# State reads in 128×32 tiles and a turn per half, batch 1 by seven half products, the scale vector loaded as rows, and the whole instruction order written anew

## The chip, the cores and the metric

One core of a Trainium2 chip. The metric is the device time in microseconds of one execution. Five engines work side by side, each through its own instructions in order: TensorE (PE, with its weight loads listed as PEld), VectorE (DVE), ScalarE (ACT), GpSimd (POOL) and SyncE (SP, which here only issues DMAs).

## The reference, cut to what matters

```python
def _attn_ref(x, state):                     # x: (8, 8, 512, 64), state: (8, 8, 32, 64)
    scores = scale * np.matmul(x, state.transpose(0, 1, 3, 2))
    a = softmax(scores)                      # over the 32 states of a head
    xread = np.matmul(a, state)
    scores2 = scale * np.matmul(state, x.transpose(0, 1, 3, 2))
    a2 = softmax(scores2)                    # over the 512 tokens
    sread = np.matmul(a2, x)
    return np.concatenate([xread, sread], axis=2)

def _moe_ref(x, w_in, w_out, alpha):         # x: 8*544 rows of 512
    h = x @ w_in                             # to 2048
    g = np.maximum(h, 0.0) + alpha * np.minimum(h, 0.0)
    return g @ w_out                         # back to 512
```

Inputs and output are float32. The output has 4352 rows of 512: for each of 8 batches 512 token rows and then 32 state rows.

## The kernel before, in words

The kernel is a list of steps in a fixed order. `ORDER` is a string of tokens such as `F.3.12.0`; the loop at the end splits each at its dots and calls the step of that name. An engine runs its instructions in the order in which the tokens issue them, so the string is a schedule of all engines at once. Nothing is planned at run time. The tokens end in an engine letter (`a` ACT, `v` DVE, `p` POOL) where a step can run on several, and in PSUM bank numbers where a step opens a bank.

**Attention.** Per batch `b`, x is loaded in f16 (`lx`, line 157, on POOL's DMA queue; batch 0 in float32 on SP's queue and cast, `cx`), transposed (`xd` by DMA, or `xt` on PE and `xo` out of PSUM), and the scores of all 8 heads are made in 64×32 tiles of the PE (`sc`, line 303). The softmax over the states is `sb`, `smax`, `ssh`, `sexp`, `ssum`, `snorm`, `wb`; for batch 0 it goes by halves, with `tsc`, `at` and `ao` around it. The softmax over the tokens is `tm`, `nb`, `te`, `tsum`, `tn`, then a DMA transpose `tt`. The state rows are loaded and transposed by `lst`, `stc`, `stt`, `sto`, `sbd`, `str`, `sro`. `rd` (line 467) then makes the state reads of a batch: 32 matmuls with x as the stationary operand (128 rows, 64 columns) and 32 columns of weights moving, two column halves of the PE in turn; `rdo` copies them into `XS`, the moving operand of the state rows' first product.

**MLP.** The first product is folded with the attention: `m` (line 494) makes state times w_in per batch and quarter of d_ff, and `F` (line 543; `f` line 565 for half batches) multiplies it by the attention weights, giving 128 rows of h for 512 tokens. "Batch 8" stands for the 256 state rows of all batches; its `F.8` (line 552) takes `XS`. `N` (lines 596 and 580, ACT) and `G` (lines 599 and 584, DVE) are the activation: ACT makes relu(-h), DVE adds (1 - alpha) times it to h. `oma` makes 1 - alpha.

**The second product** is done in two ways. Batches 0 and 1 go straight: `S` (line 613) is two matmuls of 512 columns, 32 such steps per batch, and `O` copies a finished 128×512 block out. Batches 2 to 7 and 8 go by seven half products instead of eight: `W` (line 656, POOL) makes four differences of w_out's quarters once, `U` (line 680, POOL) makes four sums of g's halves per batch in two pieces each, `P` (line 701) is four matmuls of 256 columns, 28 such steps per batch, `K` keeps a partial result out of PSUM, and `Q` (lines 732 and 734) adds or copies a quarter of the output and sends it off.

`Z` (line 223) is `fill`: matmuls on a constant pattern whose result is not used. `x_out`, `states_out`, `tokens_out` and the other copies take their engine from the token.

Of the kernel before, what the change touches and what calls it, by code (L numbers as in the profile page):

```python
# [8 lines left out]
F32 = mybir.dt.float32  # L9
F16 = mybir.dt.float16  # L10
# [11 lines left out]
xt.1.1.1.0 xt.1.0.0.3 wo.3 te.0.1 tsum.0 xo.1.0.0.v oma mo.0.0.a.0 m.1.0 f.0.1.0.4 sexp.0.1 ssum.0.1 xo.1.1.1.v  # L22
mo.1.0.a n.0.1.0 xt.1.0.1.1 xo.1.0.1.v f.0.0.0.2 n.0.0.0 xt.1.1.0.5 xo.1.1.0.v g.0.1.0.1 g.0.1.0.0 m.2.0.3.0 m.1.1
mo.1.1.a snorm.p.0.1 at.1.1 mo.2.0.a.0 ao.1.v g.0.0.0.1 m.0.1.5.4 mo.0.1.a.0 sc.1 tm.1 f.0.1.1.1 f.0.0.1.3 mo.0.1.a.1
F.0.4.5 F.0.5.4 mo.2.0.a.1 n.0.0.1 nb.1.a n.0.1.1 sb.1 te.1.0 g.0.0.0.0 g.0.1.1.0 te.1.1 S.0.2.1.0 g.0.1.1.1 F.0.6.2
N.0.6 g.0.0.1.1 g.0.0.1.0 tsum.1 G.0.6 N.0.5 G.0.5 S.0.2.0 S.0.1.1.1 m.0.2 mo.0.2.a F.0.7.3 N.0.7 smax.1 S.0.1.0 N.0.4
G.0.4 F.0.10.2 N.0.10 m.0.3 G.0.7 mo.0.3.a F.0.11.4 G.0.10 N.0.11 G.0.11 F.0.9.5 m.1.3 N.0.9 G.0.9 F.0.13.3 N.0.13
tn.0.1.p F.0.8.2 S.0.1.5 F.0.12.4 S.0.3.1.5 S.0.2.5 N.0.8 G.0.13 N.0.12 ssh.p.1 wo.1 sexp.1 F.0.15.3 S.0.3.5 G.0.8
S.0.2.4 mo.1.3.a G.0.12 ssum.1.2 F.0.14.4 S.0.2.6 S.0.1.6 m.1.2 S.0.3.6 S.0.3.4 snorm.v.1 lx.2 xd.2 wb.1 tn.1.1.a
S.0.1.4 W.1.1.p S.0.2.2 S.0.1.3 F.1.3.2 tn.0.0.a tt.0 mo.1.2.a N.0.14 S.0.2.3 G.0.14 N.0.15 G.0.15 F.1.10.4 F.1.2.3  # L30
tn.1.0.p N.1.3 G.1.3 N.1.2 G.1.2 S.0.2.7 O.0.2.a tt.1 S.0.3.0 N.1.10 F.1.4.2 N.1.4 G.1.10 G.1.4 S.0.1.7 F.1.9.0
F.1.11.3 N.1.9 G.1.9 F.1.1.4 N.1.1 G.1.1 S.0.1.2 N.1.11 W.3.0.p G.1.11 S.0.3.2 F.1.6.2 N.1.6 S.0.3.7 O.0.1.a sc.2 tm.2
m.2.2.0.4 rd.0.3 mo.2.2.a.1 sb.2 mo.2.2.a.0 rdo.0.a F.1.15.1 N.1.15 W.1.0.p G.1.15 nb.2.a S.0.0.5.4 F.1.8.0 N.1.8
G.1.8 G.1.6 te.2.0 S.0.0.2 S.0.0.1 te.2.1 S.0.0.4 W.2.0.p lx.3 F.1.7.3 smax.2 ssh.p.2 F.1.14.1 F.1.5.0 S.0.0.7 F.1.0.2
W.4.0.p N.1.14 G.1.14 N.1.7 N.1.5 S.0.3.3 G.1.7 N.1.0 G.1.0 m.3.2 F.1.13.1 mo.3.2.a S.0.0.0 F.1.12.3 S.0.0.3 G.1.5
xd.3 S.0.0.6 S.1.1.2.2 S.1.0.2.0 N.1.13 G.1.13 N.1.12 tsum.2 sexp.2 O.0.0.a G.1.12 S.1.0.4 S.1.0.0 ssum.2.1 snorm.v.2
wb.2 O.0.3.a m.2.3.3.4 mo.2.3.a.1 m.2.1 mo.2.1.a S.1.0.3 S.1.1.4 mo.2.3.a.0 tn.2.0.p S.1.1.5 W.2.1.p m.3.3.5.4
# [62 lines left out]
def kernel(  # L100
# [47 lines left out]
    def engine(e):  # L148
        return nc.gpsimd if e == "p" else nc.vector

    live = {}
    xgs = {}
    x0s = []

    def load_x(b):
        xg = xgs[b] = att.tile([128, H, 2, 2, D], F16, name=f"xg_{b}", tag="xg", bufs=3)
        nc.gpsimd.dma_start(
            xg.rearrange("p k j r d -> p k j (r d)"),
            x[b].rearrange("k (j p r) d -> p k j (r d)", j=2, r=2),
        )  # L160
# [625 lines left out]
```

## Time and profile before

| what | value |
|---|---|
| device time, median of 3 | 214.17 us (214.09 to 214.41) |
| span of the profiled execution, first to last instruction | 212.2 us |
| PE busy | 203.6 us, 1974 matmuls |
| DVE busy | 174.8 us, 260 instructions |
| ACT busy | 150.3 us, 292 instructions |
| POOL busy | 165.0 us, 106 instructions |

The page gives one span, 212.2 us; the profiled execution's own device time is not listed beside it, so the 1.9 us between the span and the median stand here for what lies around a span. "Busy" is the time in which an engine has at least one instruction running. Matmuls overlap in the array, so the busy time of PE can be full while it waits; the chain view, which gives the time from one piece to the next, tells more.

### The profile page before, as it was taken

What the parts mean: (1) busy time and instruction counts of PE and PEld (TensorE: products, weight loads), DVE (VectorE), ACT (ScalarE), POOL (GpSimd) and SP (SyncE); (2) the same over time, 40 slices, a digit from 0 to 9 for tenths busy, and PEclk for the clock granted to TensorE, in tenths of its full rate; (3) what the DMA queues carried; (4) which work ended last, traced back from release to release, by engine and by line L of the source; (5) the groups of instructions that cost most, each with busy time, mean ns of one, the idle gap of its engine ahead of it and who ended that gap; (6) DMA issues with size and microseconds to landing.
All of it is one profiled execution on the core that took longest, in us unless ns stands there. A gap on an engine that the chain in (4) does not pass through costs nothing.

```text
span 212.2 us, 4985 instructions
## 1 busy us (share of the span) xinstructions
PE 203.6 (96%) x1974; PEld 132.5 (62%) x1974; DVE 174.8 (82%) x260; ACT 150.3 (71%) x292; POOL 165.0 (78%) x106
## 2 busy tenths in 40 slices
PE   7989899989999999999999999999999999999993
PEld 5655234444444545766668776767777678888882
DVE  0789999889999999999999999899997997423221
ACT  2489998789999869987998578878773866312110
POOL 8343074946749898969989999799979995999960
PEclk9999999999999999999999999999999999999999
DMA  6999979879599299634115581141305200121142
GB/s 172 208 183 205 207 114 163 127 186 114 172 111 258 29 150 149 151 78 123 53 49 57 95 249 48 21 131 21 82 8 145 102 0 0 53 99 49 43 158 99
DMA packets 52438, 23.68 MB, mean 112 GB/s; under 512 B 38464, under 2 KB 51392, under 8 KB 52416
## 3 DMA queue, kind: packets, MB, share of 16 engines
q0 software_dynamic: 18816, 8.09, 30.2%
q1 hardware_dynamic: 33328, 15.22, 28.5%
q8 instruction: 15, 0.25, 0.4%
q10 hardware_dynamic: 272, 0.07, 0.1%
q14 instruction: 7, 0.06, 0.1%
HBM read 17.31 MB, written 8.91 MB: 124 GB/s over the span
## 4 chain that ended last, share of the span: by engine, by line
PE 86%; DVE 6%; ACT 4%; DMA 2%; issue 1%; POOL 0%; POOLq 0%; ACTq 0%; DVEq 0%; SPq 0%
PE h L543 23%; PE px L701 21%; PE o L613 11%; PE pv L701 10%; PE py L701 5%; PE m_ps L494 4%; PE fill L223 4%; PE h L552 3%; PE sr_ps L467 2%; DMA e2T<-e 2%; DVE mx L368 1%; DVE g L599 1%; ACT m L520 1%; PE sc L303 1%; PE xT_ps L288 1%; ACT neg L596 1%
## 5 line engine op out<-in xcount | busy, mean ns | idle before, releaser
L599 DVE SCALAR_TENSOR_TENSOR g<-neg,oma_sb,h 128x512 f16<-128x512 f32 (+1 forms) x140 | 92.5, 710 | 9.5 <-ACT neg L596 8.3
L596 ACT ACTIVATE neg<-h 128x512 f32<-128x512 f32 (+1 forms) x140 | 75.3, 583 | 22.3 <-PE h L543 13.3
L543 PE MATMUL h<-aT,m 128*128 128x512 f16 x248 | 67.7, 379 | 1.3 <-DVE g L599 0.6
L701 PEld LDWEIGHTS <-gsum 128*128 128x128 f16 x416 | 40.3, 98 | 11.5 <-issue 1.3
L543 PEld LDWEIGHTS <-m 128*128 128x128 f16 x248 | 23.4, 98 | 20.1 <-issue 3.3
L701 PEld LDWEIGHTS <-g 128*128 128x128 f16 x312 | 30.3, 98 | 8.7 <-issue 0.8
L680 POOL TENSOR_TENSOR gsum<-g,g 128x1024 f16<-128x1024 f16 (+1 forms) x14 | 27.8, 1986 | 7.1 <-DVE g L599 4.8
L613 PE MATMUL o<-w_out_sb,g 128*128 128x512 f16 x128 | 33.1, 379 | 0.0
L680 POOL TENSOR_TENSOR gsum<-g,gsum 128x1024 f16<-128x1024 f16 (+1 forms) x14 | 27.8, 1991 | 1.9 <-PE px L701 1.6
L680 POOL TENSOR_TENSOR gsum<-g 128x1024 f16<-128x1024 f16 (+1 forms) x14 | 27.7, 1993 | 1.9 <-issue 1.9
L680 POOL TENSOR_TENSOR gsum<-gsum,g 128x1024 f16<-128x1024 f16 (+1 forms) x14 | 27.8, 1989 | 1.0
L701 PE MATMUL px<-ws,gsum 128*128 128x256 f16 x208 | 28.0, 273 | 0.0
L373 POOL TENSOR_TENSOR ts<-ts,mx 128x1024 f32<-128x1024 f32 x7 | 13.4, 1911 | 11.9 <-DVE mx L368 11.9
L613 PEld LDWEIGHTS <-g 128*128 128x128 f16 x128 | 12.2, 98 | 15.6 <-issue 1.2
L520 ACT CAST m<-m_ps 128x512 f16<-128x512 f32 x35 | 19.3, 598 | 3.7 <-PE m_ps L494 3.6
L717 ACT COPY kept<-px 128x512 f32<-128x512 f32 (+1 forms) x16 | 9.0, 566 | 14.1 <-PE px L701 11.0
L734 DVE TENSOR_TENSOR oq<-pv,kept 128x512 f32<-128x512 f32 (+1 forms) x14 | 9.1, 650 | 10.1 <-PE pv L701 7.2
L701 PE MATMUL pv<-ws,gsum 128*128 128x256 f16 x104 | 14.8, 273 | 0.0
L701 PE MATMUL px<-w_out_sb,g 128*128 128x256 f16 x104 | 14.6, 273 | 0.0
L701 PE MATMUL px<-w_out_sb,gsum 128*128 128x256 f16 x104 | 14.6, 273 | 0.0
L701 PE MATMUL py<-w_out_sb,g 128*128 128x256 f16 x104 | 14.5, 273 | 0.0
L701 PE MATMUL pv<-ws,g 128*128 128x256 f16 x104 | 14.3, 273 | 0.0
(74 smaller groups left out, 258.4 us busy)
## 6 DMA issues: line engine op xcount, KB each, us to landing
out_dram<-oq SPq DMA_DIRECT2D x24, 256.0 KB, 2.1
xg<-in_x_dram POOLq DMA_DIRECT2D x7, 512.0 KB, 6.1
w_in_sb<-in_moe_w_in_dram POOLq DMA_DIRECT2D x4, 512.0 KB, 14.3
w_out_sb<-in_moe_w_out_dram POOLq DMA_DIRECT2D x4, 512.0 KB, 14.0
out_dram<-osb SPq DMA_DIRECT2D x8, 256.0 KB, 3.1
x<-in_x_dram SPq DMA_DIRECT2D x2, 512.0 KB, 4.9
out_dram<-oq SPq DMA_DIRECT2D x4, 128.0 KB, 2.1
st<-in_state_dram POOLq DMA_DIRECT2D x1, 224.0 KB, 8.1
```

The lines of the kernel that those rows point to most:

```text
L223: nc.tensor.matmul(t, pattern[:, :128], pattern, start=True, stop=True)
L373: engine(e).tensor_tensor(blocks(cols(live["ts", b], j, S)), blocks(scored(b, j)), over_blocks(cols(live["mx", b], j, S // N)), ALU.subtract,)
L494: nc.tensor.matmul(t[N * k : N * (k + 1), :], st_head(b, h)[64 * r : 64 * r + 64, :], w_in_sb[64 * r : 64 * r + 64, c, 512 * f : 512 * (f ...
L520: copier(e)(m_tile(b, f)[:, g, :], t[g])
L543: nc.tensor.matmul(h.rearrange("p (r j s) -> p r j s", r=2, j=2), ms[b, f][:, g, 128 * j : 128 * (j + 1)], weights(b, g), start=(g == 0), ...
L596: nc.scalar.activation(neg, h, RELU, bias=0.0, scale=-1.0)
L599: nc.vector.scalar_tensor_tensor(g_tile(b, jc), negs.pop((b, jc)), oma_sb[:, jc : jc + 1], hs.pop((b, jc)), ALU.mult, ALU.add,)
L613: nc.tensor.matmul(outs[b, q], g_tile(b, jc)[:, 128 * q : 128 * (q + 1)], w_out_sb[:, jc, :], start=not begun and jc == 2 * jc2, stop=left ...
L680: engine(e).tensor_tensor(t, x(), y(), op)
L701: nc.tensor.matmul(pbanks[b, name][:, i, :], of(b, c)[:, j, 128 * i : 128 * (i + 1)], moving[:, 4 * c + j, :], start=not begun and j == 0, ...
L717: copier(e)(t, pbanks[b, "x"])
L734: nc.vector.tensor_tensor(osb, pbanks[b, name], kept[b, add], ALU.add)
```

## The change

Five things change in the code, and the order of everything.

1. `rd` swaps its operands: the weights are stationary (128 rows, 32 columns, four column places of the PE) and x moves, 64 columns. The result has the states on the partitions, so a new step `rt` turns four batches at once with 16 matmuls on the identity, and `rto` copies 128×512 into `XS`. `rt` and `rto` run twice. `XS` keeps batch before state.
2. Batch 1's second product goes by seven half products: 32 `S` and 4 `O` become 28 `P`, 8 `U`, 3 `K` and 4 `Q`.
3. alpha is loaded as 64 rows of 32 values by four DMAs and turned by a DVE transpose, instead of one DMA of 2048 single values.
4. `fill` is 512 columns wide; the opening fill has 6 matmuls (before 16), a later `Z` one (before three), and there are 10 `Z` tokens in both.
5. Batch 0's two x loads have the first state load between them on SP's queue; batch 1's tokens are laid out so that a partition reads four tokens in a row.

In the new order 15 of the 64 `U` run on DVE (before all 56 on POOL): 10 of 128×1024 and, in batch 8, 5 of 128×512. `K` runs on DVE once (before five times), `rdo` three times (before never), `sro` not at all (before once), `mo` twice (before three times).

```diff
 ORDER = """
-wi.0 cx.0.1.a Z.0.3 cx.0.0.v Z.0.3 cx.1.0.v stc.a Z.0.3 stt.0 xt.0.0.1.1 Z.2.3 xt.0.0.0.2 cx.1.1.a xt.0.1.1.3 sbd.1.v
-lst lx.1 wi.1 wo.0 wi.2 xt.0.1.0.4 sbd.0.a xo.0.0.1.v tsc.0.1.5 xo.0.0.0.v tsc.0.0 wi.3 sto.v sc.0.0 xo.0.1.1.a
-xo.0.1.0.v sc.0.1 smax.0.0 ssh.v.0.0 sexp.0.0 tsc.1.0.1 Z.2.3 tm.0 Z.2.3 m.0.0.2.0 Z.3.3 mo.0.0.a.1 ssum.0.0 Z.3.3
-str.0.3 Z.4.3 tsc.1.1 str.1.4 nb.0.a te.0.0 sro.0.a smax.0.1 sro.1.v ssh.v.0.1 snorm.p.0.0 at.0.5 wo.2 ao.0.v
...
-Q.8.1.1 P.8.4.0.1 P.8.4.0.0 Q.8.1.0 U.8.4.1.p P.8.3.0.1 Q.8.0.0 U.8.4.0.p P.8.3.0.0 Z.0.3 Q.8.0.1.a
+stc.a Z.1.1 Z.2.1 lst Z.3.1 cx.0.1.v stt.4 sto.v xt.0.0.1.5 cx.0.0.a xt.0.0.0.0 wi.0 Z.1.1 lx.1 xo.0.0.1.a cx.1.0.a
+Z.2.1 sbd.0.v sbd.1.v tsc.0.1.3 xo.0.0.0.v tsc.0.0 cx.1.1.a smax.0.0 str.0.4 ssh.v.0.0 sro.0.a xt.0.1.1.1 sexp.0.0
+xo.0.1.1.v str.1.5 xt.0.1.0.2 Z.0.1 oma xo.0.1.0.v sc.0.0 m.0.0.3.4 sro.1.a sc.0.1 ssum.0.0 m.2.0.1.0 wi.1 mo.0.0.a.0
+Z.2.1 tm.0 nb.0.v tsc.1.0.5 tsc.1.1 smax.0.1 wo.0 snorm.p.0.0 mo.2.0.a.1 at.0.3 ssh.v.0.1 mo.0.0.v.1 mo.2.0.a.0 ao.0.v
...
+P.7.3.1.1 P.7.3.1.0 Q.7.1.1 P.7.4.1.0 P.7.4.1.1 N.8.10 G.8.10 G.8.11 U.8.1.0.v U.8.2.0.v P.7.4.0.1 P.7.4.0.0 Q.7.1.0
+K.8.1.a U.8.2.1.p P.8.6.0.1 P.8.6.0.0 P.7.3.0.0 K.8.2.a P.8.2.0.0 P.8.5.0.0 P.8.5.0.1 Q.7.0.1.a U.8.3.1.p U.8.3.0.v
+P.8.7.0.0.3 U.8.4.1.v K.8.4.v P.8.7.0.1 Q.8.1.1 U.8.4.0.p P.8.3.0.0 Q.8.0.0 P.8.3.0.1 Q.8.0.1.v P.8.4.0.1 P.8.4.0.0
+Q.8.1.0 Z.2.1
 """
...
+    TOKENS = ("j p r", "p j r")
...
-            x[b].rearrange("k (j p r) d -> p k j (r d)", j=2, r=2),
+            x[b].rearrange(f"k ({TOKENS[b == 1]}) d -> p k j (r d)", j=2, r=2),
...
-    load_x0()
+    load_x0(0)
...
-    nc.scalar.dma_start(st0_32, rows[:n0, :].rearrange("(g p) d -> p g d", p=128))
-    alpha_sb = consts.tile([128, n_jc], F32)
-    nc.sync.dma_start(alpha_sb, moe_alpha.rearrange("(jc p) -> p jc", p=128))
-    pattern = consts.tile([128, 256], F16)
+    nc.sync.dma_start(st0_32, rows[:n0, :].rearrange("(g p) d -> p g d", p=128))
+    load_x0(1)
+    alpha_rows = consts.tile([128, 32], F32)
+    nc.vector.memset(alpha_rows, 0.0)
+    alpha_quarters = moe_alpha.rearrange("(jc q c) -> q jc c", q=4, c=32)
+    for q in range(4):
+        nc.sync.dma_start(alpha_rows[32 * q : 32 * q + n_jc, :], alpha_quarters[q])
+    pattern = consts.tile([128, 512], F16)
...
-    XS = consts.tile([128, n_c, 2, N, B // 2], F16)
+    XS = consts.tile([128, n_c, 2, B // 2, N], F16)
+    reads = XS[:, :, 1].rearrange("p c b n -> p c (b n)").rearrange("p b (g d) -> p b g d", g=2)
...
-        t = single(k, f"fill_{len(zs)}", [128, 256], F32)
+        t = single(k, f"fill_{len(zs)}", [128, 512], F32)
...
-    fill(0, 16)
+    fill(0, 6)
...
-        nc.vector.tensor_scalar(oma_sb, alpha_sb, -1.0, 1.0, ALU.mult, ALU.add)
+        alpha_cols = consts.tile([128, 32], F32)
+        nc.vector.transpose(alpha_cols, alpha_rows)
+        nc.vector.tensor_scalar(oma_sb, alpha_cols[:, :n_jc], -1.0, 1.0, ALU.mult, ALU.add)
...
-        t = live["sr", b] = single(bk, f"sr_ps{b}", [128, n_c, N], F32)
-        for c in range(n_c):
-            g = c // 2
+        t = live["sr", b] = single(bk, f"sr_ps{b}", [128, 2, D], F32)
+        for g in range(2):
             for q in range(n_q):
                 r, j = divmod(q, 2)
-                for i in range(2):
-                    h = 2 * c + i
-                    k = (h - 4 * g) ^ g
+                for k in range(4):
                     nc.tensor.matmul(
-                        t[D * i : D * (i + 1), c, :],
-                        xgs[b][:, h, j, r, :],
+                        t[N * k : N * (k + 1), g, :],
                         e2T[:, g, q, N * k : N * (k + 1)],
+                        xgs[b][:, 4 * g + (k ^ g), j, r, :],
                         start=(q == 0),
                         stop=(q == n_q - 1),
+                        tile_position=(0, N * k),
+                        skip_group_check=True,
+                    )
+
+    def state_reads_out(b, e):
+        copier(e)(reads[:, b % 4], live.pop(("sr", b)))
+
+    def reads_turned(half, bk):
+        t = live["rt", half] = single(bk, f"rt_ps{half}", [128, n_c, B // 2, N], F32)
+        for g in range(2):
+            for i in range(2):
+                columns = ident.rearrange("p (c k n) -> p k c n", k=2, n=N)[:, i ^ g]
+                for b in range(B // 2):
+                    nc.tensor.matmul(
+                        t[D * i : D * (i + 1), 2 * g : 2 * g + 2, b, :],
+                        reads[:, b, g, :],
+                        columns,
+                        start=True,
+                        stop=True,
                         tile_position=(0, D * i),
                         skip_group_check=True,
                     )
 
-    def state_reads_out(b, e):
-        copier(e)(XS[:, :, b // 4, :, b % 4], live.pop(("sr", b)))
+    def reads_turned_out(half, e):
+        copier(e)(XS[:, :, half], live.pop(("rt", half)))
...
-        return rows.rearrange("b n d -> n b d")
+        return rows
```

More of the change, by code (lines that the diff above doesn't have):

```diff
@@ L23 @@
[L23 to L37, printed above, removed]
@@ new lines @@
+N.4.8 m.6.0 mo.6.0.a m.6.1.0.3 mo.6.1.a.1 G.4.8 mo.6.1.a.0 P.3.6.1.1 P.3.6.1.0 K.3.2.a rd.4.5 rdo.4.v sc.6 tm.6
+m.6.2.1.3 mo.6.2.a.1 mo.6.2.a.0 m.7.3.2.5 mo.7.3.v.1 mo.7.3.a.0 P.3.2.1.1.0 tsum.5 P.3.5.1.1 ssh.p.5 F.4.10.3 N.4.10
+P.3.5.0.1 F.4.11.1 N.4.11 P.4.2.1.1.5 U.3.4.1.p sb.6 G.4.10 smax.6 P.3.2.0.0 G.4.11 P.3.5.1.0 F.4.3.2 P.4.2.0.1
+P.3.2.1.0 sexp.5 ssum.5.3 nb.6.a te.6.1 snorm.v.5 U.3.3.0.p P.3.5.0.0 P.3.7.0.0.1 N.4.3 K.3.4.a P.3.2.0.1 G.4.3
+P.3.3.1.0 U.3.3.1.p ssh.p.6 wb.5 sexp.6 P.3.3.0.0 P.3.3.1.1 te.6.0 P.3.7.0.1 P.3.7.1.1 Q.3.0.0 P.4.2.0.0 P.3.7.1.0
@@ L624, in out_rows @@
         r, j = divmod(q, 2)
-        return out[b * S2 : b * S2 + S, :].rearrange("(j p r) d -> r j p d", j=2, r=2)[r, j]
+        return out[b * S2 : b * S2 + S, :].rearrange(f"({TOKENS[b == 1]}) d -> r j p d", j=2, r=2)[r, j]
     def second_out(b, q, e):
@@ L721, in quarter_rows @@
         if b < B:
-            rows = out[b * S2 : b * S2 + S, :].rearrange("(j p r) d -> r p j d", j=2, r=2)
+            rows = out[b * S2 : b * S2 + S, :].rearrange(f"({TOKENS[b == 1]}) d -> r p j d", j=2, r=2)
             return rows[th, :, :, cols]
         rows = out.rearrange("(b s) d -> b s d", s=S2)[4 * th : 4 * (th + 1), S:, cols]
-        return rows.rearrange("b n d -> n b d")
+        return rows
     def quarter_out(b, th, dh, e=None):
```

147 lines of the change are left out of this document (78 added, 69 removed).

## The prediction

> **What bounds the kernel now.** I read the page first, then the chain in order of time, then who waits on PE, then the engines by ten-microsecond windows.
>
> ```profile
> PE 203.6 (96%) x1974; PEld 132.5 (62%) x1974; DVE 174.8 (82%) x260; ACT 150.3 (71%) x292; POOL 165.0 (78%) x106
> PE 86%; DVE 6%; ACT 4%; DMA 2%; issue 1%; POOL 0%; POOLq 0%; ACTq 0%; DVEq 0%; SPq 0%
> ```
>
> ```profile
> 1.24 3.61 PE fill L223 x16
> 15.87 0.60 PE h L565 x4
> 24.15 1.41 DVE g L599 x2
> ...
> 31.49 0.86 PE o L613 x4
> 47.47 1.29 PE h L543 x6
> 56.91 0.61 PE sr_ps L467 x32
> 80.50 0.87 PE px L701 x8
> 110.48 0.56 PE m_ps L494 x16
> 207.39 0.89 PE px L701 x8
> ```
>
> ```profile
> PE h L543 <- DVE g L599: 0.6, 2, 0.3
> ```
>
> The chain lists a start, a length and the work. From about 31 us to 208.3 us (207.39 + 0.89) it is nearly all matmuls end to end at the same prices: 512 columns 0.215 us (0.86 / 4 and 1.29 / 6), 256 columns 0.109 us (0.87 / 8). The waits of the main product add up to 0.6 us. So PE is streaming, and a column taken off it moves the end by its own time. Before 31 us the chain changes between fills, DVE and ACT: there the latency of the first batch decides. After 208.3 us come the last copy and its DMA, 3.9 us, and they stay.
>
> ```profile
> 20.00:30.00 10.00, 8.81 (x60) 3.17 (x59) 9.94 (x17) 9.95 (x21) 3.23 (x3) 1.00 1.06 176
> 30.00:40.00 10.00, 10.00 (x54) 4.36 (x53) 9.07 (x12) 8.28 (x14) 6.05 (x5) 1.00 0.97 129
> 40.00:50.00 10.00, 9.28 (x95) 4.22 (x94) 9.20 (x12) 8.49 (x20) 5.35 (x4) 1.00 1.15 182
> 50.00:60.00 10.00, 10.00 (x124) 4.46 (x124) 9.90 (x14) 9.45 (x17) 8.22 (x6) 1.00 0.47 115
> 60.00:70.00 10.00, 10.00 (x61) 4.41 (x60) 9.63 (x16) 9.71 (x21) 7.42 (x5) 1.00 1.30 197
> ...
> 180.00:190.00 10.00, 10.00 (x94) 8.97 (x92) 2.96 (x6) 2.73 (x7) 9.84 (x6) 1.00 0.16 55
> 190.00:200.00 10.00, 10.00 (x94) 8.96 (x92) 3.77 (x8) 2.02 (x5) 9.92 (x7) 1.00 0.15 53
> 200.00:210.00 10.00, 8.56 (x77) 7.27 (x75) 3.02 (x7) 1.71 (x4) 4.92 (x5) 1.00 0.40 141
> ```
>
> The columns after the length are the busy times of PE, PEld, DVE, ACT and POOL. DVE is nearly full while PE streams: 174.8 - 2.96 - 3.77 - 3.02 = 165.0 us lie before 180 us. POOL has gaps early and none at the end. Two engines thus stand close behind PE, and the change loads both.
>
> **Batch 1's second product.** It loses 64 matmuls of 512 columns, 64 x 0.215 = 13.8 us, and gains 28 steps of 4 matmuls of 256 columns, 112 x 0.109 = 12.2 us. PE: **-1.6 us**. What comes with it:
>
> ```profile
> L680 POOL TENSOR_TENSOR gsum<-g 128x1024 f16<-128x1024 f16 x12 | 25.4, 2133 | 1.9 <-issue 1.9
> L680 POOL TENSOR_TENSOR gsum<-g 128x512 f16<-128x512 f16 x2 | 2.3, 1152 | 0.0
> L734 DVE TENSOR_TENSOR oq<-pv,kept 128x512 f32<-128x512 f32 x12 | 8.2, 688 | 7.3 <-PE pv L701 4.3 <-issue 2.8
> L717 ACT COPY kept<-px 128x512 f32<-128x512 f32 x14 | 8.3, 593 | 10.6 <-PE px L701 10.6
> L393 DVE TENSOR_TENSOR an<-ts,r 128x1024 f16<-128x1024 f32 x7 | 8.5, 1219 | 0.2
> L478 ACT CAST XS<-sr_ps 128x128 f16<-128x128 f32 x8 | 3.6, 455 | 0.7 <-PE sr_ps L467 0.5
> ```
>
> Eight sums on POOL, 8 x 2.13 = 17.1 us; three additions on DVE, 3 x 0.69 = 2.1 us; on ACT three keeps and one output of 0.59 us in place of four output copies of that size, nothing. SP's four output transfers of the batch stay four of 256 KB, nothing. The 17.1 us are covered by POOL's gaps of 30 to 70 us (40 - 27.0 = 13.0 us) and of 20 to 30 us (6.8 us), into which the new order moves the first `W`. That cover is thin, and it is a rival below.
>
> **State reads.** Today 32 matmuls go two abreast in 0.61 us. The fixed part of such a burst I take from `m`: 16 matmuls of 512 columns in eight places are two rounds of 0.215 us, and take 0.56 us, so 0.13 us is entry. Then a pair of reads costs (0.61 - 0.13) / 16 = 0.030 us. The new form has 8 rounds of four. Lower bound: a round costs its 64 columns, a quarter of 0.109 us, so 8 x 0.027 + 0.13 = 0.35 us. Upper bound: nothing overlaps, 32 x 0.027 + 0.13 = 1.0 us. I take 8 x 0.030 + 0.13 = 0.37 us, because the rows of `m` and of today's reads both show column places working side by side. Eight batches: 8 x (0.37 - 0.61) = **-1.9 us** (bounds -2.1 and +3.1). The price of a pair, 0.030 us, is more than the 32 / 256 x 0.109 = 0.014 us of its moving columns. The Trainium skill (TensorEngine Tiling (Array Packing), Performance Considerations) says that a matmul has an overhead of about 60 cycles on this chip, so that one moving column costs as much as 60; by that rule the pair's price agrees, and a round of 64 columns costs nearly what one of 32 does.
>
> **The turn.** Twice 16 matmuls of 64 columns. Four in a row share a column half, so I count them one after the other: 16 x 0.027 + 0.13 = 0.56 us, twice 1.1 us; were they two abreast it would be 2 x (8 x 0.030 + 0.13) = 0.7 us. I take **+1.1 us**. The same page (Key Properties) says that changing the tiling mode drains the array, which speaks against adding two bursts; the 0.13 us of entry is where that would show. The two copies behind the turns, about 0.6 us each on ACT by the 512-element row above, have `P` steps beside them. The read copies were 0.455 us on ACT; three go to DVE, where 128 elements lie between nothing and the 0.69 us of 512; I take 0.25 us, 0.8 us in all.
>
> **The start.** The first half-batch products wait on one chain; DVE's place in it is copying.
>
> ```profile
> 5.18 0.43 DVE L173 CAST xg<-x 128x512 f16<-128x512 f32 x1 [4.04 <-DMA x<-in_x_dram]
> 12.55 1.05 POOL L393 TENSOR_TENSOR an<-ts,r 128x512 f16<-128x512 f32 x1 [5.14 <-DVE r L390]
> 13.65 0.40 PE L354 MATMUL at_ps<-ident,an 128*128 128x128 f16 x4
> 13.79 1.13 DVE L270 COPY stT<-st_ps 128x896 f16<-128x896 f16 x1
> 14.71 0.62 PE L288 MATMUL xT_ps<-ident,xg 128*128 128x128 f16 x8 [0.67 <-DMA xg<-in_x_dram]
> 15.40 0.42 DVE L357 COPY aT<-at_ps 128x512 f16<-128x512 f16 x1
> ```
>
> ```profile
> st<-in_state_dram POOLq DMA_DIRECT2D x1, 224.0 KB, 8.1
> alpha_sb<-in_moe_alpha_dram SPq DMA_DIRECT2D x1, 8.0 KB, 11.1
> ```
>
> The transposed weights are ready at 14.05 us, but DVE copies them at 15.40 us because 1.13 us of state copies stand in front. In the new order both state copies are on ACT, which may take them early since the state load is issued before w_in; against that DVE gets a shift, a 0.69 us `mo` and the small transpose of alpha ahead of that copy. Counting every DVE step ahead of it at the rows' durations gives 9.1 us before and 8.6 us after: -0.5 us. Batch 1's x, which PE waits for at 14.71 us (0.67 us), arrives in runs twice as long and without alpha's 2048 single values: up to -0.7 us. I take **-0.7 us** for both (bounds -2 and +1). Fills fall from 16 + 27 half-width to 6 + 9 full-width matmuls ahead of steady work. The opening 16 cost 0.226 us each (3.61 / 16) against 0.109 us later, so they run at half rate; six double ones take 2.7 us of 3.6 us, with three more behind them. I cost that at nothing, since the cast at 5.18 us comes later; if the array then stayed at half rate until 15 us, some 2 us of bursts would double, +2 us.
>
> **The queues moved past.** The load of the first states goes from ACT's queue to SP's, behind the first half of x, and the second half behind it; SP's four alpha issues come after both. POOL's w_in and w_out issues are spread further apart, w_in's third behind a softmax step. Nothing asks for these weights before `m` of that quarter, so nothing is costed; were the alpha rows late, DVE would stop at `oma` with the first `tm` behind it, which the +1 us bound above holds.
>
> **The sum.** -1.6 - 1.9 + 1.1 - 0.7 = -3.1 us on the span of 212.2 us: 209.1 us. The median of 214.17 us is 1.9 us above that span, so **211.1 us**.
>
> **The rivals.** *DVE becomes the bound (slower).* Fifteen sums move from POOL to DVE.
>
> ```profile
> 195.33 1.26 DVE L599 SCALAR_TENSOR_TENSOR g<-neg,oma_sb,h 128x256 f16<-128x256 f32 x3 [2.68 <-ACT neg L596]
> ```
>
> Today DVE's last activation ends at 196.6 us with 3.8 us of DVE work behind it, so 171.0 us up to it. Apart from the sums the moves net -1.8 us (batch 1's additions +2.1, reads +0.8, four keeps -2.8, a state copy -1.1, one `mo` -0.7, small ones -0.1). In the new order 13 `P` steps, 5.7 us, follow the last activation, so with PE's end at 205.2 us it has to end by 199.5 us. DVE idles 15.0 us before 180 us; the rest is 184.5 us. Room: 184.5 - 169.2 = 15.3 us for the 11 sums ahead of that point, 1.39 us each. No row shows such a sum on DVE. The nearest, 1024 elements at one price, is 1.22 us; 512 elements of two operands are 0.69 us; if it also waits for a whole POOL sum it is 1.22 + 2.13 = 3.35 us. I take 1.22 us, which uses 12.9 us of 15.3 us (ten whole ones and a half one) and moves nothing. It decides above 1.39 us: with POOL busy six tenths of that stretch (41 us of its steps in some 65 us) and half a POOL sum of wait at each meeting, 11 x 0.64 = 7.0 us come on top, 2.4 us are room, **215.7 us**. The Trainium skill (SBUF — State Buffer, Who interferes with whom) states this wait: a DVE instruction with two SBUF inputs and a GpSimd instruction that reads SBUF exclude each other for a whole instruction. Its page VectorE: DVE Perf Modes (the perf-mode tier table) speaks the other way: a 16-bit sum in SBUF runs at double rate, 1224 ns for 2048 elements; by that a sum would be near 0.69 us and the wait would fit. No run here shows either yet.
>
> *POOL becomes the bound in batches 1 and 2.*
>
> ```profile
> L373 POOL TENSOR_TENSOR ts<-ts,mx 128x1024 f32<-128x1024 f32 x7 | 13.4, 1911 | 11.9 <-DVE mx L368 11.9
> L157 POOL DMA_DIRECT2D xg<-in_x_dram x7 | 8.4, 1203 | 2.9 <-PE sr_ps L467 2.9
> ```
>
> Idle from 20 to 70 us is 19.7 us (6.8 + 13.0), against 17.1 us of new sums, 2.6 us to spare; but POOL waits in its order, 11.9 us for maxima and 2.9 us for buffers over the run, and batch 1's products stand early, with batch 2 behind them. If 5.6 us of such waits recur in that stretch, POOL is 3 us late and PE waits: **214.1 us**, a gain handed back.
>
> *The reads do not overlap* (the change doesn't do what it says): 211.1 + 5.0 = **216.1 us**.
>
> *More at the start*: two microseconds more of the fills and DVE turns before 31 us go away, **209 us**.
>
> **How the numbers follow.** Forecast 0.58, POOL 0.14, DVE 0.13, reads 0.05, more at the start 0.10. A measurement tells 0.2%, 0.43 us, from no change. Faster: 0.58 + 0.10 + 0.05 of POOL's = 0.73; same 0.04 and slower 0.05 from the rest of POOL's; with DVE and reads slower is 0.23. The range leaves out the upper half of DVE's and the reads' cases and the lowest of the start's: 208.2 to 215.5 us. The forecast's own range is 209.5 to 212.9 us.
>
> **What would show it.** A read burst near 0.37 us and a turn near 0.56 us; batch 1's `P` at 0.109 us per matmul; the first half-batch h near 15.2 us; PE's last `P` near 205 us; DVE's sums at 0.7 to 1.2 us. It is wrong if the waits view of PE shows microseconds on POOL's sums or on DVE's activations after 40 us, or if a sum on DVE lasts 2 us.

## The result, and the profile after

| what | before | after |
|---|---|---|
| device time, median | 214.23 us (214.09 to 214.41, 4 runs) | 221.62 us (220.25 to 223.06, 4 runs) |
| ratio to before | | 1.034 [1.029, 1.039] |
| profiled execution: time, span | span 212.2 us | 220.91 us, span 219.1 us |

The change makes the kernel 3.4% slower; the forecast was 211.1 us, and 221.6 us lies beyond its range. Some executions of the changed kernels run at half rate for a while, for a cause that the third group of experiments finds; ratios leave the most disturbed ones out. The page after, engines' busy times and then the shares of the chain that ended last:

```profile
PE 197.6 (90%) x2024; PEld 132.1 (60%) x2024; DVE 185.7 (85%) x278; ACT 150.3 (69%) x294; POOL 156.7 (72%) x101
PE 66%; DVE 12%; DMA 8%; ACT 5%; issue 3%; POOL 2%; DVEq 0%; POOLq 0%; ACTq 0%
```

PE's share of the chain fell from 86% to 66%, and DVE's and DMA's rose from 6% and 2% to 12% and 8%. Part of that is only another path through the start: 12.58 us of DMA's share are one load of w_in that the chain follows from 4.26 us, where it followed fills and copies before, and the time lost up to 31 us did not grow (below). The rest says that PE is not streaming any more; something makes it stand. To see where, I priced every matmul at its streaming row (0.215 us for 512 columns, 0.109 us for 256, the bursts at their chain pieces) and called the rest of the time up to the end of the last half product lost:

| | before | after |
|---|---|---|
| priced work of PE | 191.7 | 188.8 |
| lost, 0 to 31 us | 14.3 | 14.2 |
| lost, 31 to 50 us | 1.1 | 0.3 |
| lost, 50 to 57 us | 0.0 | 1.4 |
| lost, 57 to 128 us | 0.6 | 0.1 |
| lost, 128 to 152 us | -0.1 | 5.3 |
| lost, 152 us to the last half product's end | 0.6 | 0.7 |
| the last half product's end | 208.3 | 210.9 |
| from there to the end of the span | 4.0 | 8.2 |

PE's work fell by 2.9 us, half a microsecond more than the 2.4 us forecast (1.6 + 1.9 - 1.1). Against that stand 5.5 us more of standing still, and 4.2 us more behind the last half product. Both are in the views. First the windows view of both kernels, columns as before (before, then after):

```profile
50.00:57.00 7.00, 7.00 (x83) 2.90 (x84) 6.90 (x11) 6.55 (x11) 6.30 (x4) 1.00 0.64 160
128.00:152.00 24.00, 24.00 (x260) 17.04 (x258) 23.15 (x33) 21.00 (x44) 22.44 (x13) 1.00 0.25 67
```

```profile
50.00:57.00 7.00, 5.73 (x61) 2.97 (x60) 6.93 (x9) 6.02 (x12) 6.97 (x4) 1.00 1.03 163
128.00:152.00 24.00, 19.29 (x194) 13.10 (x192) 21.84 (x28) 14.42 (x30) 17.49 (x12) 1.00 0.43 89
```

Then the chain of the kernel after, in order of time:

```profile
4.26 12.58 DMA w_in_sb<-in_moe_w_in_dram
...
49.50 5.43 DMA xT<-xg
...
75.00 0.63 PE sr_ps L475 x64
...
132.00 2.19 DVE gsum L707
134.19 0.67 DVE g L626
134.85 0.04 issue
134.90 0.59 PE h L570 x2
...
141.43 2.39 DVE gsum L707
143.82 0.67 DVE g L626
144.49 0.04 issue
144.53 0.61 PE h L570 x2
...
156.90 0.40 PE rt_ps L494 x16
...
210.04 0.89 PE pv L728 x8
```

At 134.9 and 144.5 us PE has waited for an activation on DVE, and the activation stands behind a sum that lasted 2.2 and 2.4 us. The waits view has three such waits:

```profile
PE h L570 <- DVE g L626: 4.7, 3, 2.0
```

The two behind the sums are 1.4 and 1.3 us. The third and longest, 2.0 us at 149.7 us, stands behind no sum; it is taken up under "What was still lost". The sums by form show two prices; engine, shapes, count, then busy time and mean nanoseconds:

```profile
L707 DVE TENSOR_TENSOR gsum<-g,g 128x1024 f16<-128x1024 f16 x3 | 3.8, 1277 | 0.0
L707 DVE TENSOR_TENSOR gsum<-g 128x1024 f16<-128x1024 f16 x1 | 2.3, 2275 | 0.0
L707 DVE TENSOR_TENSOR gsum<-g,gsum 128x1024 f16<-128x1024 f16 x3 | 2.1, 686 | 0.2 <-PE px L728 0.2
```

And the timeline tells what makes the price, DVE's rows first and POOL's behind them:

```profile
131.91 2.27 DVE L707 TENSOR_TENSOR gsum<-g 128x1024 f16<-128x1024 f16 x1
141.35 2.47 DVE L707 TENSOR_TENSOR gsum<-g,g 128x1024 f16<-128x1024 f16 x1
131.52 2.12 POOL L707 TENSOR_TENSOR gsum<-g,gsum 128x1024 f16<-128x1024 f16 x1
141.14 2.12 POOL L707 TENSOR_TENSOR gsum<-g 128x1024 f16<-128x1024 f16 x1
```

A sum on DVE takes 0.69 us by itself. One that is issued while POOL is in a sum waits for that sum's end: POOL's from 131.52 ends at 133.64, and DVE's, begun at 131.91, ends 0.54 us later. Three of the ten whole ones were caught (the third at 190.24 us). The Trainium skill (SBUF — State Buffer, Who interferes with whom) has this exclusion for a DVE instruction with two SBUF inputs; the trace agrees.

For the end, the wait of SP's queue and the DMA issues of the kernel after (the last figure of the second line is missing, where the page before has 2.1 us to the landing):

```profile
SPq L808 <- DMA out_dram<-oq: 5.4, 1, 5.4
out_dram<-oq SPq DMA_DIRECT2D x4, 128.0 KB
```

and the DMA view's GB/s in slices, before for 206 to 214 us and after for 208 to 218 us:

```profile
GB/s 384 348 31 0 0 0 0 123 384 149 0 0 0 0 0 169 399 87 87 394 174 36 364 251 5 0 0 0 0 0 0 0 0 0 0 0 0 0 0 41
```

```profile
GB/s 201 0 254 336 324 78 12 16 20 8 0 16 37 20 94 86 82 86 94 74 37 98 90 94 78 90 90 94 94 98 98 78 70 98 98 98 82 21 0 0
```

Before, a 128 KB transfer of batch 8 is a burst of over 350 GB/s. After, the four run one behind the other mostly at 90 to 98 GB/s, a quarter of that, up to 217.5 us.

### The profile page after: what moved, and what is told of

Read it like the earlier page. It is cut to its first block, busy times and chain, and to the rows that moved or that the text cites. A ratio compares the mean times of both kernels' runs of the same rounds, so it can differ in the third digit from the quotient of the medians.

```text
span 219.1 us, 5100 instructions
## 1 busy us (share of the span) xinstructions
PE 197.6 (90%) x2024; PEld 132.1 (60%) x2024; DVE 185.7 (85%) x278; ACT 150.3 (69%) x294; POOL 156.7 (72%) x101
## 4 chain that ended last, share of the span: by engine, by line
PE 66%; DVE 12%; DMA 8%; ACT 5%; issue 3%; POOL 2%; DVEq 0%; POOLq 0%; ACTq 0%
PE h L570 20%; PE px L728 19%; PE pv L728 10%; DMA w_in_sb<-in_moe_w_in_dram 6%; PE py L728 5%; DVE g L626 5%; PE o L640 4%; DVE gsum L707 3%; PE h L579 3%; PE m_ps L521 3%; DMA xT<-xg 2%; ACT neg L623 2%; ACT m L545 2%; PE sr_ps L475 1%; DVE nb L424 1%
## 5 line engine op out<-in xcount | busy, mean ns | idle before, releaser
L728 PEld LDWEIGHTS <-gsum 128*128 128x128 f16 x480 | 46.3, 98 | 13.1 <-issue 2.0
L728 PEld LDWEIGHTS <-g 128*128 128x128 f16 x360 | 34.9, 98 | 11.1 <-DVE g L626 0.9
L728 PE MATMUL px<-ws,gsum 128*128 128x256 f16 x240 | 32.6, 273 | 0.0
L707 POOL TENSOR_TENSOR gsum<-g,gsum 128x1024 f16<-128x1024 f16 (+1 forms) x12 | 24.5, 2049 | 9.8 <-PE px L728 5.8
L707 POOL TENSOR_TENSOR gsum<-g,g 128x1024 f16<-128x1024 f16 x11 | 23.3, 2122 | 4.9 <-DVE g L626 4.9
L707 POOL TENSOR_TENSOR gsum<-gsum,g 128x1024 f16<-128x1024 f16 (+1 forms) x12 | 24.5, 2044 | 1.6 <-DVE gsum L707 1.1
L744 ACT COPY kept<-px 128x512 f32<-128x512 f32 (+1 forms) x23 | 13.2, 575 | 10.4 <-PE px L728 10.3
L640 PE MATMUL o<-w_out_sb,g 128*128 128x512 f16 x64 | 16.9, 379 | 0.0
L728 PE MATMUL px<-w_out_sb,g 128*128 128x256 f16 x120 | 16.2, 273 | 0.2 <-DVE g L626 0.2
L728 PE MATMUL px<-w_out_sb,gsum 128*128 128x256 f16 x120 | 15.9, 273 | 0.0
L728 PE MATMUL pv<-ws,g 128*128 128x256 f16 x120 | 15.9, 273 | 0.0
L545 ACT CAST m<-m_ps 128x1024 f16<-128x1024 f32 x13 | 13.9, 1067 | 0.7 <-PE m_ps L521 0.7
L459 POOL TENSOR_SCALAR e<-e,r 128x512 f16<-128x512 f16 x12 | 8.2, 685 | 7.5 <-DVE r L451 7.5
```

The source lines that it names most:

```text
L459: nc.gpsimd.tensor_scalar(e2, e2, r2, 1.0, ALU.mult, ALU.mult)
L545: copier(e)(m_tile(b, f), t)
L640: nc.tensor.matmul(outs[b, q], g_tile(b, jc)[:, 128 * q : 128 * (q + 1)], w_out_sb[:, jc, :], start=not begun and jc == 2 * jc2, stop=left ...
L707: engine(e).tensor_tensor(t, x(), y(), op)
L728: nc.tensor.matmul(pbanks[b, name][:, i, :], of(b, c)[:, j, 128 * i : 128 * (i + 1)], moving[:, 4 * c + j, :], start=not begun and j == 0, ...
L744: copier(e)(t, pbanks[b, "x"])
```

## The experiments

Every ratio is against the kernel before, run on the same chip.

### The end: the order of batch 8's rows

The changed `XS` has batch before state, so a transfer of batch 8 has 4 batches as its outermost dimension, where it had 32 states. The first run undoes that in the kernel after, the second does it alone in the kernel before.

```diff
-    XS = consts.tile([128, n_c, 2, B // 2, N], F16)
+    XS = consts.tile([128, n_c, 2, N, B // 2], F16)
...
-        return rows
+        return rows.rearrange("b n d -> n b d")
```

> The changed kernel with batch 8's rows put back to state before batch, in XS and in the output transfers; nothing else. In the changed kernel PE ends at 210.8 us and the last four transfers of 128 KB run until 217.5 us, against 208.3 and 210.9 us before. Theory A (the transfer's outermost run of 4 instead of 32 leaves only few DMA engines to carry it): the four transfers take 1.8 us after their issue as before, the stretch from PE's end to the span's end falls from 8.3 us to 3.9 us, and the time to about 217.2 us. Theory B (the tail is only the new order of the last steps): no change, about 221.6 us.

Measured: 220.96 us (218.64 to 221.77), ratio 1.034 [1.030, 1.038]. In the profiled execution the tail behind the last half product is 4.2 us instead of 8.2 us, and its DMA line has a landing time again:

```profile
out_dram<-oq SPq DMA_DIRECT2D x4, 128.0 KB, 2.1
```

But its last half product ended at 214.4 us instead of 210.9 us, so the median moved by only 0.7 us. Where those 3.5 us went is the third group.

> The kernel before with batch 8's rows in the changed kernel's order (batch before state), in XS and in the output transfers; nothing else. Theory A (few DMA engines carry a transfer whose outermost run is 4): the stretch from PE's end to the span's end grows from 3.9 us to about 8 us, 218.4 us. Theory B: no change, 214.2 us.

Measured: 217.17 us (216.81 to 217.26), ratio 1.013 [1.010, 1.016]; the last half product ends at 208.2 us (208.3 us before), and the tail is 7.1 us instead of 4.0 us. The edit alone costs 3.0 us, all of it behind the last half product. The Trainium skill (DMA: Bandwidth & Descriptors, Why a DMA increments its semaphore by 16 and not by 1) says that a transfer is spread over the largest number of engines, at most 16, that divides the outermost dimension of both its sides: with 4 that is at most 4, with 32 it can be 16. The quarter of the rate agrees.

### The middle: sums on DVE or on POOL

```diff
-... U.4.3.1.v ... U.5.1.1.v ... U.8.4.1.v ...
+... U.4.3.1.p ... U.5.1.1.p ... U.8.4.1.p ...        (all 15)
```

> The changed kernel with all 15 sums that it gives to VectorE given back to GpSimd, at the same places in the order. Theory A (a sum on VectorE waits for a running GpSimd sum, and this makes VectorE the pace between 128 and 152 us, where PE loses 5.3 us more than before): VectorE loses 11 us of work, PE's lost time in that stretch falls to under 1.5 us, and the time to about 217 us, unless GpSimd, now with 27 us more, comes late. Theory B (GpSimd could not have carried them; it becomes the pace in batches 5 to 8): the loss only moves to products that wait for GpSimd's sums, and the time is 221 to 226 us.

Measured: 226.54 us (225.03 to 228.07), ratio 1.057 [1.050, 1.064]. The wait behind the first caught sum is gone (0.2 us are lost from 128 to 140 us), but 2.4 us are lost between 140 and 152 us, 1.9 us from there to 185 us and 3.6 us behind 200 us. Behind 195 us PE waits for POOL:

```profile
PE px L728 <- POOL gsum L707: 3.0, 2, 2.2
```

The second half of batch 0's x landed late in this execution, as below, and PE waits 4.3 us for its cast, where it waits 0.7 us in the kernel after. With all 64 sums POOL comes late as well.

> Both of the above. If the two causes are separate, their effects add: about 212.5 us under theory A of both. If GpSimd becomes the pace, 217 to 221 us.

Measured: 219.86 us (217.58 to 223.11), ratio 1.022 [1.014, 1.030]. With state before batch, all sums on POOL come out near the kernel with 15 on DVE (220.96 us). So the same 15 tokens cost 4.9 us in the one pair (226.54 against 221.62 us) and gain 1.1 us in the other. All four kernels have the loads by which half of x can land late, so these two runs do not settle what the 15 sums are worth in the new order. What both profiled executions show is that the waits do not go away: PE waits 3.5 us for POOL's sums in each.

The same 15 tokens alone, in the kernel before, where they stand at other places in the order:

```diff
-... U.4.3.1.p ... U.5.1.1.p ... U.8.4.1.p ...        (the same 15)
+... U.4.3.1.v ... U.5.1.1.v ... U.8.4.1.v ...
```

> The kernel before with the same 15 sums of halves moved from POOL to DVE as in the changed kernel, nothing else. Theory (a sum on DVE waits for a POOL sum that is running, whole): a sum of 128x1024 lasts 0.68 us alone and 2.3 to 2.5 us where it meets one; three to five such meetings, and since DVE is nearly full up to 190 us the last matmul moves by 2 to 5 us: 216 to 219 us. Rival (the sums at 0.68 us fit DVE's idle time and POOL is relieved of some 28 us): 213.5 to 214.3 us.

Measured: 225.43 us (223.17 to 226.15), ratio 1.050 [1.046, 1.054], over twice the cost that I expected. Four sums are caught (2.23, 1.41, 2.16 and 2.42 us), which is 5.5 us above 0.68 us each. The rest is a queue: a sum on DVE stands in DVE's order, behind additions that wait for PE, and POOL's next sums need its result. The waits of POOL:

```profile
POOL gsum L680 <- DVE gsum L680: 22.1, 4, 8.7
```

Two half-rate windows follow PE's standstills at 188 and 199 us. So moving these sums is a loss by itself at the places that they have in the old order, and the 5.5 us of the caught sums are only half of the 11 us that it costs.

### The start: the first loads and the array's clock

The profiled execution of the first run above ran at half rate from 12.8 to 16.2 us. My first suspect were the fewer fills.

```diff
-    fill(0, 6)            # and one of 512 columns per Z
+    fill(0, 16)           # and three of 256 columns per Z
```

> The changed kernel with batch 8 state before batch (as in the run of that edit alone, 220.96 us) and with the fills of the kernel before: 256 columns, 16 in the opening, three per Z. Theory (the shorter fills let the clock of the matrix unit fall to half for 3.4 us windows in the start, in some executions): no half-rate record before 20 us, the clock at 0.995 or more, no scatter over 1 us, and about 217 us (the last matmul at 210.8 us as in the changed kernel's profiled execution, 4.4 us of tail, 1.9 us around the span). Rival (the new order's idle time of the matrix unit in the start does it, whatever the fills): the same half-rate records, 219 to 222 us.

Measured: 220.06 us (216.14 to 222.99); the scatter and the half-rate windows (11.3 to 18.2 us) stay. The theory fell.

> The kernel before with the fills of the changed one alone: 512 columns, 6 in the opening, one per Z. Theory: with fewer fills half-rate records appear between 5 and 20 us in some executions, the times scatter by over 1 us, median 215 to 217.5 us. Rival (what the prediction said, the fills cost nothing): the clock stays full, 214.2 us.

Measured: 213.43 us (213.02 to 214.11), ratio 0.996 [0.994, 0.997], at full clock throughout. The new fills are a small gain of 0.8 us.

What the half-rate executions share is the second half of batch 0's x: its casts began at 11.1 to 12.5 us (four profiled executions), against 8.1 us in the profiled execution of the kernel after and 6.7 us before. In the change the first states' load stands between the two halves on SP's queue. The next run takes the kernel with state before batch and puts the loads back.

```diff
-    load_x0(0)
+    load_x0(0)
+    load_x0(1)
...
-    nc.sync.dma_start(st0_32, rows[:n0, :].rearrange("(g p) d -> p g d", p=128))
-    load_x0(1)
+    nc.scalar.dma_start(st0_32, rows[:n0, :].rearrange("(g p) d -> p g d", p=128))
```

> The changed kernel with batch 8 state before batch and with the first loads where the kernel before has them: both halves of batch 0's x first on SP's queue, the first states on ACT's. Its own fills stay. Theory (the second half of x, third on SP's queue, lands at 8 us in one execution and at 11 to 12 us in others; the matrix unit then stands still for most of one window of 3.4 us and is granted half rate in the next): the second half lands at 6.5 to 7 us, no half-rate record before 30 us, clock 0.99 or more, and 215.5 to 217.5 us. Rival (the halves are late because of the POOL queue's state load ahead of w_in, not of SP's order): still 8 us or more, half-rate windows stay, 219 to 221 us.

Measured: 216.73 us (216.31 to 218.12), ratio 1.013 [1.010, 1.016], 4.2 us below the run without this edit. The second half's casts begin at 7.3 us, and no half-rate window is left in the start. The same edit, the other way round, in the kernel before:

> The kernel before with one edit: the first states' load moved from ACT's queue to SP's, between the two halves of batch 0's x, as in the changed kernel. Theory: the second half of x lands later, at 7.5 to 12 us instead of 6.7, and where the matrix unit's busy share of a 3.4 us window falls under a half, a half-rate window follows: 215 to 219 us with scatter. Rival (the place on SP's queue costs the 0.6 us of one issue): 214.2 to 214.8 us.

Measured: 220.20 us (219.49 to 221.22), ratio 1.027 [1.025, 1.030]: one DMA's place costs 6.0 us. First the chain, then the windows view cut where the clock changes:

```profile
1.88 10.76 DMA x<-in_x_dram
```

```profile
5.41:8.82 3.41, 2.52 (x23) 1.40 (x21) 0.00 (x0) 0.01 (x1) 1.92 (x3) 1.00 1.23 206
8.82:12.23 3.41, 0.00 (x0) 0.00 (x0) 0.00 (x0) 0.00 (x0) 0.00 (x0) 1.00 2.06 178
12.23:15.65 3.42, 2.31 (x53) 2.01 (x54) 2.88 (x8) 1.57 (x3) 0.00 (x0) 0.50 1.49 196
15.65:19.06 3.41, 3.24 (x21) 1.46 (x18) 2.58 (x4) 1.73 (x4) 0.64 (x1) 0.50 1.22 203
```

The second half was issued 0.6 us later (1.88 us against 1.27 us), yet could be used 6 us later, at 12.7 us: by then the state load on its own queue and POOL's large loads are ahead of it, and 178 to 206 GB/s are moving meanwhile. Which of these loads holds it up was not taken apart. PE stands for a whole window and is granted half rate (0.50, the column after POOL's busy time) in the next two. The Trainium skill (TensorE: Matmul & The Clock Gate, Part 1) gives a free-running window of 3413 ns; the records agree, 3.41 us each. It speaks of an idle window, and here much less is enough. With state before batch and the old loads, the windows around 147 us:

```profile
146.70:150.11 3.41, 1.41 (x10) 0.72 (x9) 3.38 (x6) 1.29 (x3) 1.22 (x2) 1.00 0.00 0
150.11:153.53 3.42, 3.42 (x13) 1.48 (x11) 2.58 (x4) 1.76 (x4) 3.42 (x3) 0.50 0.65 156
```

PE was busy for 1.41 of 3.41 us, 0.41, and the next window ran at half rate. In all profiled executions here but one (the last point of this document), windows at full rate with a share from 0.00 to 0.43 were followed by half rate, and those with 0.47 (behind the last product of the run of the reads alone), 0.50 (in the run below) and more were not; at half rate windows with 0.78 and less were followed by another, and one with 0.95 was the last. That fits the scatter of the times: by this, where a window falls on a standstill decides over half a window's work, an estimated 1.7 us.

### The two caught sums

```diff
-... U.4.3.1.v ... U.5.1.1.v ...
+... U.4.3.1.p ... U.5.1.1.p ...
```

> The run of the changed kernel with state before batch and the old first loads, and two of the 15 sums on DVE (batch 4's fourth and batch 5's first, the two that met a POOL sum at 132 and 141 us and lasted 2.3 and 2.5 us) back on POOL. Theory (the lock sets the pace there): the matrix unit's lost time between 128 and 152 us falls from some 5 us to 2 us or less, and the time by 1.5 to 3 us below that run. Rival (POOL has no room either, as with all sums on POOL, 226.5 us): lost time 4 us or more between 128 and 185 us, no faster than that run.

Measured: 214.41 us (213.91 to 216.59), ratio 1.003 [1.001, 1.006], 2.3 us below the run without this edit. PE's lost time from 128 to 152 us falls from 5.9 to 3.0 us; the two sums' waits were 4.75 - 2 x 0.69 = 3.4 us. The windows view, without and with the edit (POOL, the fifth busy time, takes them):

```profile
128.00:152.00 24.00, 19.30 (x190) 12.97 (x188) 21.78 (x28) 14.26 (x29) 17.50 (x12) 0.96 0.45 91
```

```profile
128.00:152.00 24.00, 21.45 (x238) 14.79 (x238) 19.68 (x30) 16.41 (x33) 23.90 (x15) 1.00 0.48 95
```

Some of the fall is the half-rate window from 150.11 us, which only the first of these two profiles has (0.96 against 1.00 in the clock's column). So the caught sums are about half of the loss there; the 2.0 us wait named above stays.

### The reads alone

The code of `rd`, `rt` and `rto` as in the change, state before batch kept; in the order:

```diff
+rt.0.2 rto.0.a          (behind the reads of batch 3)
-rd.7.5 F.7.10.0 F.7.6.1 rdo.7.a F.8.13.4 N.7.10 G.7.10 F.8.2.5 N.7.6 ...
+rd.7.5 F.7.10.0 rdo.7.a F.7.6.1 P.5.4.1.1 rt.1.5 rto.1.a N.7.10 G.7.10 N.7.6 ...
```

> The kernel before with the state reads in 128x32 tiles and the two turns, nothing else (the second turn needs batch 8's first steps moved behind it by five matmul groups). Theory (these terms of the prediction hold, at the changed kernel's measured prices): 8 x (0.33 - 0.61) + 2 x 0.40 = -1.4 us, 212.8 us. Rival (the matrix unit's saving is given back, since DVE and POOL set the pace): 214.2 us; worse than 214.5 us if the turn's wait for the last reads' copy stops the matrix unit.

Measured: 217.56 us (216.43 to 219.00), ratio 1.015 [1.011, 1.018]. PE's priced work fell by 1.4 us as expected, but 5.1 us are lost between 152 and 185 us. The copy behind the turn stands ahead of two activations on ACT, and PE waits for what DVE makes of them:

```profile
PE h L483 <- DVE g L539: 1.7, 1, 1.7
```

A window there with a busy share of 0.43 brings a half-rate one. The second try puts the turn behind those activations and takes the shorter fills as well:

```diff
+rd.7.5 F.7.10.0 F.7.6.1 rdo.7.a P.5.4.1.1 N.7.10 G.7.10 F.7.15.2 N.7.6 Q.5.1.0 G.7.6 rt.1.5 rto.1.a ...
```

> The kernel before with the reads in 128x32 tiles, the two turns and the shorter fills; the second turn now stands behind the last products of batch 7 that are ready, so that ACT and DVE take those first. Theory (the 5 us that the first try lost between 152 and 185 us were that pinch and the half-rate window behind it): 213.4 - 1.4 = 212.0 us. Rival (the reads' saving is given back in any place, since DVE sets the pace in the middle): 213.4 us or more.

Measured: 214.42 us (213.73 to 214.94), ratio 1.000 [0.998, 1.002]. No half-rate window is left, but 1.7 us are still lost between 152 and 185 us, most of it behind the turn, and the time is 1.0 us above that of the shorter fills alone (213.43 us). So the reads' 1.4 us were not to be had in the old order with either of my two places for the turn; the rival held.

### What was still lost

With three edits undone the time is 214.4 us, not 211. In the waits of PE (around 53 us, then from 125 to 155 us) and of DVE (the same 30 us) these were left:

```profile
PE sc L314 <- DMA xT<-xg: 0.9, 1, 0.9
...
PE h L570 <- DVE g L626: 2.0, 1, 2.0
...
DVE ts L346 <- ACT e L441: 2.7, 1, 2.7
```

DVE stands 2.7 us for ACT's second exponential of batch 7, with the activation behind it for which PE waits.

```diff
-te.7.0 F.6.2.5 mo.7.2.a.1 mo.7.2.a.0 F.6.14.4 N.6.2 te.7.1 sb.7
+te.7.0 te.7.1 F.6.2.5 mo.7.2.a.1 mo.7.2.a.0 F.6.14.4 N.6.2 sb.7
```

> The 214.41 us run of the changed kernel (state before batch, old first loads, two sums back on POOL) with one more edit: the second exponential of batch 7's token softmax moved ahead of two copies and one activation on ACT. Theory (the loss at 140 to 152 us is of the order: DVE stands 2.7 us for that exponential, with the activation behind it that PE waits 2.0 us for): that wait goes, PE's lost time between 140 and 152 us falls from 2.4 to under 1 us, the half-rate executions at 216 us go, 212.5 to 213.2 us. Rival (DVE and POOL have no room there whatever the order): the wait moves on, 214 us or more.

> The same kernel as in the run with four mends, for a profile at full rate: 212.8 to 213.1 us, lost time of the matrix unit between 140 and 152 us under 1 us, no half-rate window.

Measured: 212.96 us (212.74 to 213.00 in four executions; a fifth, with a clock of 0.56 throughout, took 339.4 us), ratio 0.992 [0.991, 0.994], and again 212.85 us (212.47 to 212.93), ratio 0.993 [0.991, 0.995]. That is 1.5 us for one token's place; PE's lost time from 140 to 152 us is 0.8 us (2.4 us before the edit), and of the other eight executions none is near 216 us.

```diff
-U.2.3.0.p sc.4 tm.4 sb.4 m.5.3.5.3 ... P.1.4.0.0 P.1.4.1.1
+U.2.3.0.p m.5.3.5.3 P.1.4.0.0 P.1.4.1.1 sc.4 tm.4 sb.4 ...
```

> As the run with four mends, and batch 4's scores put 0.9 us of matmuls later, since they stand 0.9 us for the DMA transpose of x at 53 us. Theory: PE's lost time between 50 and 57 us falls from 0.9 to near 0, and the time by 0.5 to 0.9 us below the run with four mends. Rival (the later scores delay batch 4's softmax, which comes out later as a wait elsewhere): no change.

Measured: 213.69 us (213.03 to 213.92), ratio 0.995 [0.994, 0.996], 0.7 us slower. I had moved the wrong batch's scores: those at 53 us are batch 3's. The wait stayed, and 1.2 us were lost anew between 70 and 85 us. With the right ones:

```diff
-sc.3 tm.3 m.4.0.2.1 mo.4.0.a.1 U.1.2.1.p mo.4.0.a.0 P.1.1.0.0 sb.3 P.1.1.1.0
+m.4.0.2.1 P.1.1.0.0 P.1.1.1.0 sc.3 tm.3 mo.4.0.a.1 U.1.2.1.p mo.4.0.a.0 sb.3
```

> As the run with four mends (212.96 us), and batch 3's scores behind one more 0.22 us of state times w_in and 0.9 us of batch 1's half products. Theory: the wait for the DMA transpose at 53 us goes from 0.9 to 0.3 us or less and the time to 212.0 to 212.6 us. Rival (batch 3's softmax, 1.1 us later, is waited for instead): 213 us or more.

Measured: 211.88 us (211.66 to 211.91), ratio 0.989 [0.987, 0.991]. It beats both kernels. Its page and two of its windows:

```profile
PE 198.9 (95%) x2024; PEld 132.4 (63%) x2024; DVE 181.1 (86%) x276; ACT 150.4 (72%) x294; POOL 160.6 (76%) x103
```

```profile
50.00:57.00 7.00, 7.00 (x65) 3.42 (x64) 6.87 (x9) 6.80 (x14) 6.97 (x4) 1.00 0.99 170
128.00:152.00 24.00, 23.30 (x296) 16.24 (x296) 21.52 (x33) 16.75 (x34) 24.00 (x14) 1.00 0.48 100
```

| kernel | median, us |
|---|---|
| after | 221.62 |
| + state before batch | 220.96 |
| + first loads as before | 216.73 |
| + two sums back on POOL | 214.41 |
| + second exponential earlier | 212.96, 212.85 |
| + batch 3's scores later | 211.88 |

These are medians of runs on different occasions, beside medians of before of 214.15 to 214.54 us. The first step shows 0.7 us where the tail shows 4.0 us, since the start of its profiled execution was later by about as much; in the kernel before the same edit is worth 3.0 us.

## Why the prediction was wrong, by its own steps

**What was right.** PE bounds the kernel before, and PE's columns were priced well. Batch 1's half products stream at 0.109 us, no wait for POOL's sums shows in batch 1's stretch (lost time from 57 to 128 us 0.1 us), and the rival in which POOL holds up batches 1 and 2 did not come. A read burst takes 0.63 / 2 = 0.32 us (forecast 0.37), a turn 0.40 us (0.56): the reads and the turn net -1.5 us by their old 0.61 us, where -0.8 us was forecast. The wait that I named as the sign of an error, a sum on DVE of 2 us, is the one that appeared.

**The end ("SP's four output transfers ... nothing"; the last copy and its DMA "stay").** This is the first step that failed: +4.2 us in the profiled execution, 3.0 us measured alone. I counted the bytes of the transfers and not the order of their dimensions, though `return rows` stood in the diff, and that last line was never priced.

**The queues ("nothing is costed") and the start (-0.7 us, bounds -2 to +1).** I saw that the first states' load goes between the halves of x, and priced it by when weights are asked for. The second half of x itself was not followed. In the profiled execution it cost little (first half-batch h at 15.4 us against 15.9 us before; lost time to 31 us 14.2 against 14.3 us), but in four other profiled executions with these loads the half came at 11 us or more. As a place on a queue it costs 4.2 us in the changed kernel and 6.0 us in the kernel before. The bound of +1 us was to hold late alpha rows; it lacked the other loads under way and the half-rate windows behind a standstill. The spread of w_in's issues did cost little: the chain after runs through the second of them, but PE itself waits 0.4 us for it. A single profile would not have shown this: the scatter of the times and the clock of each run did.

**The fills (nothing).** Measured alone -0.8 us, with the sign of "more at the start". The +2 us that I feared of them come from the loads.

**The sums on DVE (1.22 us each, 1.39 us of room).** The price was wrong both ways: 0.69 us alone, 2.3 to 2.5 us when caught in the kernel after. The mean over ten is 1.2 us, within the room, so the limit of 1.39 us that I set was kept, and PE waited all the same: two caught sums ten microseconds apart stop it for 1.4 and 1.3 us where batch 6's and 7's softmax fills DVE, and idle time that DVE has before 120 us doesn't help. (14 `P` steps, not 13, follow the last activation, so the room was 1.35 us each; that changes nothing here.) Room summed over 180 us is not room where it is needed. The rival that had this wait in it gave 215.7 us, and the runs put about 2.3 us on two sums.

**The new order behind the start (no term).** The sum had nothing for waits that the order itself brings after 31 us. It has 2.0 us at 149.7 us, behind an exponential on ACT, and 1.4 us for the transpose of x at 53 us; moving one token and one group of tokens brought 1.5 us and about 1 us.

**The sum.** -2.9 us of PE's work, as argued, and then +4.2 us at the end, +5.5 us of waits (5.4 us of them from 128 to 152 us, 1.4 us for the transpose of x, 1.3 us less elsewhere): +6.8 us of span, and 6.9 us was measured. With five places mended, three undone and two places of the new order moved, the kernel takes 211.88 us. That this is near the forecast proves little, since it is another kernel; what bears the arithmetic out is the -2.9 us of PE's work. The forecast was wrong about what the new places cost.

## What to carry to other kernels

Price what a diff does to the shape of each transfer, not only to its bytes: the last DMA of a kernel has nothing to hide it. When a load moves on a queue, follow that load and the ones behind it to the instruction that waits for them, and count a standstill of PE twice if it can fill most of a 3.4 us window. Room on an engine counts only in the stage where the new work lands, and a mean price hides a sum that is cheap alone and three times as dear beside another engine's.

## What the runs showed of the hardware

- A window of 3.41 us at full rate in which PE was busy for a share of 0.43 or less was followed by one at half rate in every profiled execution but that of the last point; windows with 0.47 and 0.50 were not. Full idleness is not needed.
- A load issued 0.6 us later on the same queue, behind one more, could be used 6 us later (12.7 us against 6.7 us).
- A 128 KB transfer with 4 as its outermost dimension ran at about 94 GB/s, with 32 at over 350 GB/s.
- A 128x1024 f16 sum on DVE takes 0.69 us, against 2.13 us on POOL. Begun while one on POOL runs, it ends about 0.55 us behind that one's end, and so took up to 2.48 us; a POOL sum that meets one on DVE takes up to 2.57 us.
- One execution of the version with four mends was granted a clock of 0.56 from end to end and took 339 us, where the others took 213 us; what brought it about stays open.
